# Another plan for the first batch: the flag behind the sums, filters ahead of weights, the last rows stored and read back first, eight weight blocks beside the first units

## The chip, the cores and the metric

The kernel runs on one core of a Trainium2 chip. The metric is the device time of one execution in microseconds (us), the median of three runs. The engines are named as the profile names them: PE is TensorE (matmuls), PEld its weight loads, DVE is VectorE, ACT is ScalarE, POOL is GpSimd, SP is SyncE, which issues nearly all DMAs here. Every engine works through its own list of instructions in order.

## The reference

Two stages, of which the second does most of the arithmetic:

```python
X = np.fft.rfft(x, axis=1)                    # x: 8 x 3008 x 256
y = np.fft.irfft(X * F, n=3008, axis=1)       # F: 1505 x 256, complex
h = y.reshape(24064, 256) @ w_in              # 256 x 2048
P = a[0] + a[1]*h + a[2]*h**2 + a[3]*h**3
Q = 1.0 + abs(b[0])*abs(h) + abs(b[1])*h**2
out = (P / (Q + 1e-06)) @ w_out               # 2048 x 256
```

All in float32 (the weights come as float64 bits that the kernel decodes itself). The kernel keeps float32 accuracy by splitting each operand in a high and a low part, so that one product takes three matmuls.

## The kernel before, in words

**Units.** The second stage is cut into token tiles of 512 and, in each, 16 slices of 128 of the 2048 inner columns. A pair of tile and slice is a unit; there are 752, and the last two are split. `pipeline` writes the program one unit index `i` after the other: `product_in` of unit i (six matmuls on PE, `h_u`), then its scalar functions on ACT (`act0` to `act4`), the sums on DVE (`p`, `g_hi`, `rest`, `g_lo`), two steps on POOL (`pool_q1`, `pool_m`), each with a lag in units (`ORDER`), and `product_out` of unit i-4 (six matmuls, `o`). Under the flag of the `if`, which holds for these inputs, the branch with `squares` runs.

**Convolution.** The Fourier stage of a batch is done as small DFTs. `conv_items(b)` is a generator: `stage1` (matmuls `s`), then `stage2`, whose twelve items each have a forward product `y` on PE, two multiplications with the filter on DVE, `cross` and `total`, `halves` (the split `zr`, high part on ACT, low part on POOL) and an inverse product `z` on PE, which ACT evicts to `ev`. `zr` has a single buffer. Finished quarters go to a scratch in HBM (`scr2`), and `stage3` reads chunks of it back (`tl`), multiplies by `e_sb` (matmuls `x`) and writes `xhl`, the tokens for the units. In `pipeline` a counter `credit` grows by `RATES[0]` = 0.6 a unit while batch 1 is made and by 0.38 later, and an item costs 0.86. `SPN` = 1 is the unit from which batch 1 may begin. A chunk of the batch that is still being made forces the rest of that batch at once:

```python
need = chunks[xk][0]
if c1 <= t * T + RX and ((c0 if f > XF else c1) < T * (t + 2) or need < nxt):
    if need >= nxt:
        run(gen or conv_items(nxt))
```

The first chunk of batch 1 comes up at unit 73 (tile 4, slice 9).

**Head.** Batch 0 is done ahead of the units by `head`, whose steps a small planner (`Plan`) puts in order: each step has an engine, a cost, the steps that it needs and a due time, and the planner takes the one that can begin first. Steps: loads `x0` to `x6`; `sum` (DVE) and `s` (PE); the flag (some twenty tiny POOL operations, its bits written by a DVE operation) and the reciprocals; for each of six filters a load, `sign` (POOL or ACT), `swb` (ACT), two `y`, `mul` (two DVE operations each), `z` and an eviction; stores `zst`; the read-back `tl`; and the decoding of the weight blocks in `FIRST`. A block is decoded by `magnitude` and, if in `EASED`, `scale` on ACT, four DVE operations (`guard`, `shift`, `top`, `power`), `rest` (POOL if eased, else DVE), `whole` (POOL), `upper` (ACT), `lower` (POOL). Twelve of the sixteen blocks are in `FIRST`; four are decoded beside the units listed in `LATE`. All engines take the branch of the `if` only after their part of the head.

Of the kernel before, what the change touches and what calls it, by code (L numbers as in the profile page):

```python
# [53 lines left out]
RAW = {10: "f1", 11: "f2", 14: "f1", 15: "oe"}  # L54
LATE = {0: 10, 3: 11, 6: 14, 9: 15}
# [66 lines left out]
class Plan:  # L122
# [60 lines left out]
def conv_moe(ctx: ExitStack, tc: tile.TileContext, xp, filt, w_in, w_out, mats, small, sgn, outT):  # L183
# [36 lines left out]
    def load_flag():  # L220
# [24 lines left out]
        v.tensor_tensor(out=flag_sb, in0=all_[:, :1], in1=all_[:, :1], op=ALU.mult)  # L245

    def recip_scalars():

        ts, tt = nc.gpsimd.tensor_scalar, nc.gpsimd.tensor_tensor
        yes, no = scal[:, 54:55], scal[:, 55:56]  # L250
        n, r, z, half = scal[:, :7], scal[:, 56:63], cf_sb[:, 8:15], scal[:, 63:64]
# [9 lines left out]
        v.reciprocal(r, n)  # L261
# [249 lines left out]
    class Stage2:  # L511
# [17 lines left out]

        def sign_filter(self, q, by):  # L530
            f1 = self.f[q][0]
            for k in range(4):
                out, sg = f1[64:, k], sgn_sb[64:, 4 * q + k : 4 * q + k + 1]
                if by == "A":
                    nc.scalar.activation(out, out, AF.Copy, scale=sg)
                else:
                    nc.gpsimd.tensor_scalar(out=out, in0=out, scalar1=sg, scalar2=1.0, op0=ALU.mult, op1=ALU.mult)

        def swap_filter(self, q):
            f1, f2 = self.f[q]  # L540
            nc.scalar.activation(f2[:64], f1[64:], AF.Copy)
# [128 lines left out]
    class Unit:  # L670
# [137 lines left out]
    def head():  # L808
# [30 lines left out]

        def s_sum(j):  # L840
# [320 lines left out]
```

## Time and profile before

| what | value |
|---|---|
| median of three runs | 2470.52 us (2466.96 to 2471.79) |
| the profiled execution's own time | 2470.01 us |
| its span, first to last instruction | 2468.2 us |
| PE, DVE, ACT, POOL busy | 98%, 89%, 91%, 87% |

The span is 1.8 us shorter than the execution's own time. PE is busy nearly throughout, and the four engines are all near their limits, so the time is read from the stretches in which PE is not busy.

### The profile page before, as it was taken

What the parts mean: (1) busy time and instruction counts of PE and PEld (TensorE: products, weight loads), DVE (VectorE), ACT (ScalarE), POOL (GpSimd) and SP (SyncE); (2) the same over time, 40 slices, a digit from 0 to 9 for tenths busy, and PEclk for the clock granted to TensorE, in tenths of its full rate; (3) what the DMA queues carried; (4) which work ended last, traced back from release to release, by engine and by line L of the source; (5) the groups of instructions that cost most, each with busy time, mean ns of one, the idle gap of its engine ahead of it and who ended that gap; (6) DMA issues with size and microseconds to landing.
All of it is one profiled execution on the core that took longest, in us unless ns stands there. A gap on an engine that the chain in (4) does not pass through costs nothing.

```text
span 2468.2 us, 36873 instructions
## 1 busy us (share of the span) xinstructions
PE 2419.6 (98%) x10868; PEld 1953.5 (79%) x10868; DVE 2197.2 (89%) x3571; ACT 2237.4 (91%) x4285; POOL 2147.6 (87%) x2245
## 2 busy tenths in 40 slices
PE   8799999999999999999999999999999999999998
PEld 4578877888788887888788877888788888888886
DVE  7789988989899888998899988899889998998997
ACT  6799999999999999999999999999999999888887
POOL 7888987999879987899879997899879987888897
PEclk9999999999999999999999999999999999999999
DMA  8554334432443233433343233432343210100000
GB/s 285 153 179 146 99 119 132 136 99 77 126 151 111 89 101 109 153 94 98 111 141 119 87 98 120 136 111 89 106 133 109 70 38 17 34 26 17 21 9 19
DMA packets 131698, 251.16 MB, mean 102 GB/s; under 512 B 10958, under 2 KB 78862, under 8 KB 131486
## 3 DMA queue, kind: packets, MB, share of 16 engines
q1 hardware_dynamic: 131486, 248.70, 32.3%
q8 instruction: 88, 1.44, 0.2%
q14 instruction: 124, 1.02, 0.1%
HBM read 154.12 MB, written 94.54 MB: 101 GB/s over the span
## 4 chain that ended last, share of the span: by engine, by line
PE 69%; POOL 15%; DVE 7%; issue 4%; ACT 3%; DMA 2%; SPq 0%; POOLq 0%; ACTq 0%; DVEq 0%
PE o L769 10%; PE o L770 10%; PE o L771 10%; PE h_u L689 10%; PE h_u L692 10%; PE h_u L690 10%; POOL q_u L751 6%; POOL q_u L732 4%; PE s L504 3%; PE x L648 3%; POOL zw L575 2%; DVE h_u L754 2%; PE z L414 2%; DVE hi_u L746 1%; PE y L414 1%
## 5 line engine op out<-in xcount | busy, mean ns | idle before, releaser
L751 POOL TENSOR_TENSOR q_u<-q_u,hi_u 128x512 f32<-128x512 f32 x753 | 976.5, 1297 | 197.9 <-DVE hi_u L746 175.3
L754 DVE SCALAR_TENSOR_TENSOR h_u<-h_u,q_u 128x512 f32<-128x512 f32 x753 | 521.3, 692 | 121.9 <-POOL q_u L751 120.9
L769 PE MATMUL o<-hi_u,wo_sb 128*128 128x512 f32 x1506 | 629.2, 418 | 0.0
L689 PE MATMUL h_u<-xhl,wi_sb 128*128 128x512 f32 x1506 | 591.1, 393 | 10.8 <-DVE xhl L664 5.4
L770 PE MATMUL o<-lo_u,wo_sb 128*128 128x512 f32 x1506 | 588.0, 390 | 3.2 <-DVE lo_u L760 3.2
L690 PE MATMUL h_u<-xhl,wi_sb 128*128 128x512 f32 x1506 | 586.6, 390 | 0.7 <-DVE xhl L664 0.7
L771 PE MATMUL o<-hi_u,wo_sb 128*128 128x512 f32 x1506 | 586.8, 390 | 0.0
L732 POOL TENSOR_SCALAR q_u<-q_u,scal 128x512 f32<-128x512 f32 x753 | 580.6, 771 | 2.9 <-ACT a_u L714 2.9
L697 ACT ACTIVATE q_u<-h_u 128x512 f32<-128x512 f32 x753 | 450.7, 599 | 131.8 <-PE h_u L692 104.1
L737 DVE SCALAR_TENSOR_TENSOR h_u<-w_u,scal,h_u 128x512 f32<-128x512 f32 x753 | 561.6, 746 | 0.0
L760 DVE TENSOR_TENSOR lo_u<-h_u,a_u 128x512 fp32r<-128x512 f32 x753 | 514.4, 683 | 0.1
L746 DVE SCALAR_TENSOR_TENSOR hi_u<-h_u,a_u 128x512 fp32r<-128x512 f32 x753 | 512.4, 680 | 1.7 <-ACT a_u L722 1.4
L714 ACT ACTIVATE a_u<-q_u 128x512 f32<-128x512 f32 x753 | 477.8, 635 | 0.0
L710 ACT ACTIVATE q_u<-q_u 128x512 f32<-128x512 f32 x753 | 473.0, 628 | 1.8
L692 PE MATMUL h_u<-xhl,wi_sb 128*128 128x512 f32 x1506 | 464.2, 389 | 0.0
L704 ACT ACTIVATE w_u<-h_u 128x512 f32<-128x512 f32 x753 | 446.1, 592 | 0.0
L722 ACT ACTIVATE a_u<-a_u 128x512 f32<-128x512 f32 x688 | 432.5, 629 | 0.3
L689 PEld LDWEIGHTS h_u<-xhl,wi_sb 128*128 128x128 f32 x1506 | 283.1, 188 | 80.0 <-DVE lo_u L760 15.3
L770 PEld LDWEIGHTS o<-lo_u,wo_sb 128*128 128x128 f32 x1506 | 283.6, 188 | 76.2 <-issue 17.3
L769 PEld LDWEIGHTS o<-hi_u,wo_sb 128*128 128x128 f32 x1506 | 283.3, 188 | 72.2 <-issue 18.4
L771 PEld LDWEIGHTS o<-hi_u,wo_sb 128*128 128x128 f32 x1506 | 283.0, 188 | 60.1
L690 PEld LDWEIGHTS h_u<-xhl,wi_sb 128*128 128x128 f32 x1506 | 283.2, 188 | 59.4 <-DVE xhl L664 1.1
(107 smaller groups left out, 2291.2 us busy)
## 6 DMA issues: line engine op xcount, KB each, us to landing
f<-filt SPq DMA_DIRECT2D x174, 256.0 KB
xin<-xp SPq DMA_DIRECT2D x48, 512.0 KB
scr<-ev SPq DMA_DIRECT2D x48, 512.0 KB
outT<-oe SPq DMA_DIRECT2D x46, 512.0 KB
xin<-scr SPq DMA_DIRECT2D x42, 512.0 KB
yl<-scr SPq DMA_DIRECT2D x42, 512.0 KB
scr<-xin SPq DMA_DIRECT2D x42, 480.0 KB
scr<-yl SPq DMA_DIRECT2D x42, 480.0 KB
```

What stands on the lines that cost most here:

```text
L689: nc.tensor.matmul(o, w_in_part(0, f, cc), xh[:, cc, ts], start=cc == 0, stop=False)
L690: nc.tensor.matmul(o, w_in_part(0, f, cc), xl[:, cc, ts], start=False, stop=False)
L692: nc.tensor.matmul(o, w_in_part(1, f, cc), xh[:, cc, ts], start=False, stop=cc == 1)
L732: nc.gpsimd.tensor_scalar(out=self.q, in0=self.q, scalar1=S1, scalar2=S2, op0=ALU.mult, op1=ALU.add)
L737: v.scalar_tensor_tensor(out=H, in0=w, scalar=PK, in1=H, op0=ALU.add, op1=ALU.mult)
L746: nc.vector.scalar_tensor_tensor(out=self.hi, in0=self.H, scalar=self.p0, in1=self.a, op0=ALU.add, op1=ALU.mult)
L751: nc.gpsimd.tensor_tensor(out=self.q, in0=self.q, in1=self.hi.bitcast(F32), op=ALU.mult)
L754: nc.vector.scalar_tensor_tensor(out=self.H, in0=self.H, scalar=self.p0, in1=self.q, op0=ALU.add, op1=ALU.subtract)
L760: nc.vector.tensor_tensor(out=self.lo, in0=self.H, in1=self.a, op=ALU.mult)
L769: nc.tensor.matmul(o, w_out_part(0, f, dd), self.hi, start=f == 0 and self.cols.start == 0, stop=False)
L770: nc.tensor.matmul(o, w_out_part(0, f, dd), self.lo, start=False, stop=False)
L771: nc.tensor.matmul(o, w_out_part(1, f, dd), self.hi, start=False, stop=f == 15 and self.cols.stop == T)
```

## The change

The planner's costs and due times are set anew, the flag's bits and the reciprocals become steps of their own on DVE behind the last sum, all filters are loaded as early as their tiles allow (filter 3 gets tiles of its own), and the last quarter's rows are stored in two parts, of which the first twelve of each half go first and are read back first. Eight weight blocks are decoded in the head and eight beside units 1 to 15, where `pool_q1` of the first twelve units moves from POOL to ACT. The convolution of batch 1 may begin at unit 14 (`START`), and the first chunk of `stage3` in `pipeline` is not taken at unit 1 any more. The diff, cut to its core:

```diff
-FIRST = (0, 1, 4, 5, 2, 3, 8, 9, 6, 7, 12, 13)
+FIRST = (0, 1, 4, 5, 2, 3, 8, 9)
-EASED = (0, 1, 4, 2, 8, 6, 7, 12, 10, 11, 14, 15)
+EASED = (0, 1, 4, 5, 2, 8, 6, 7, 12, 13, 10, 11, 14, 15)
+OWN = {3: 16}
+START = 14
-SOON = {0: (10, 11, 14, 15)}
+SOON = {0: (6, 7, 12, 13, 10, 11, 14, 15)}
-LATE = {0: 10, 3: 11, 6: 14, 9: 15}
+LATE = {1: 6, 3: 7, 5: 12, 7: 13, 8: 10, 10: 11, 11: 14, 13: 15}
+Q1A = 12
+DUE = 5
...
-        v.tensor_tensor(out=flag_sb, in0=all_[:, :1], in1=all_[:, :1], op=ALU.mult)
+    def flag_bits():
+        v.tensor_tensor(out=flag_sb, in0=scal[:, 54:55], in1=scal[:, 54:55], op=ALU.mult)
...
+    def stage3_load(k, k0=0, k1=K2, tl=None, issuers=(nc.sync,)):
...
         def pool_q1(self):
-            if self.squares:
+            if self.squares and self.i < Q1A:
+                nc.scalar.activation(self.q, self.q, AF.Identity, scale=S1, bias=S2)
+            elif self.squares:
                 nc.gpsimd.tensor_scalar(out=self.q, in0=self.q, scalar1=S1, scalar2=S2, op0=ALU.mult, op1=ALU.add)
...
+        def load_filter(q):
+            if q in OWN:
+                tiles = [mlp.tile([128, TT], F32, tag=slots[OWN[q] + n], name=f"fr0_{q}_{n}") for n in range(4)]
...
-        due = lambda i: 18 + 2.6 * i
+        due = lambda i: DUE + 2.6 * i
...
+        add("bits", flag_bits, "DVE", 0.2, ["flag", "sum12"], due=14)
+        add("inputs", recip_inputs, "POOL", 2.0, ["flag"], due=4)
+        add("recips", recips, "DVE", 0.25, ["inputs", "bits"], due=15)
+        add("recip_step", recip_step, "POOL", 0.9, ["recips"], due=4)
...
-            add(f"f{q}", lambda q=q: s.load_filter(q), "SP", 1.0, due=-8 + q if q < 3 else due(2 * q) - 9, moves=1.95, ring=("f1", f"z{2 * q + 1}"), twin="f2")
+            add(f"f{q}", lambda q=q: load_filter(q), "SP", 1.0, ["s12"] if q in OWN else [], due=-8 + q, moves=2.35, ring=None if q in OWN else ("f1", f"z{2 * q + 1}"), twin=None if q in OWN else "f2")
...
+        add("few", lambda: rows(5, 0, 12, (nc.sync, nc.scalar)), "SP", 0.5, ["zev11"], due=-7, moves=0.3)
+        add("zst5", lambda: rows(5, 12, N1, (nc.sync, nc.sync)), "SP", 1.0, ["tr0!", "tr1!"], due=-5, moves=1.3)
...
+        def rows(q, r0, r1, issuers):
+            for e, issuer in enumerate(issuers):
+                p = slice(e * N1 + r0, e * N1 + r1)
+                issuer.dma_start(scr2[0][4 * q : 4 * q + 4, p].rearrange("k p c -> p k c"), s.ev[q][p])
...
+            add(f"tr{k}", lambda k=k: tl_rest(k), "SP", 0.8, [f"tl{k}!", "few", "zst4"], due=-6 + k, moves=0.3)
...
+            decode(i, 0, "magnitude", "scale")
             step(0, "product_in")
...
-            if i < n and f in (XF, XF + 8) and not xgen and xk < len(chunks):
+            if i < n and f in (XF, XF + 8) and i > XF and not xgen and xk < len(chunks):
...
-                if gen is None and nxt < B and i >= SPN and i >= 94 * nxt - 94 - EARLY:
+                if gen is None and nxt < B and i >= START and i >= 94 * nxt - 94 - EARLY:
```

What this does to the order of instructions is shown at three places. The first is DVE at the start, where `xs` are the sums, `xin` the loaded tiles and L245 (L253 in the changed kernel) writes the flag's bits. Before:

```order
L447 TENSOR_TENSOR xs_124<-xin_0_109 120x512 [waits DMAHW0_49]
L447 TENSOR_TENSOR xs_128<-xin_0_109 120x512
L245 TENSOR_TENSOR scal<-scal 128x1 [waits Pool_49]
L447 TENSOR_TENSOR xs_166<-xin_1_112 120x512 [waits DMAHW2_49]
L447 TENSOR_TENSOR xs_180<-xin_1_112 120x512
```

And now, at the end of the sums:

```order
L462 TENSOR_TENSOR xs_292<-xin_6_122 120x256 [waits DMAHW7_49]
L462 TENSOR_TENSOR xs_292<-xin_6_122 120x256
L253 TENSOR_TENSOR scal<-scal 128x1 [waits Pool_49]
L271 RECIPROCAL scal<-scal 128x7 [waits Pool_49]
L925 TENSOR_TENSOR f_0_152<-y_0_344,f_0_152 128x512 [waits DMAHW2_49,PE_49,Activation_49]
```

The operation that waits for POOL stood behind the second sum and now stands behind the fourteenth, ahead of the first multiplication with a filter.

The second place is SP's list behind filter 2, where `f` and `fr` are filters, `raw` weight blocks and `scr` the scratch. Before:

```order
L524 DMA f_2_213<-filt 64x1024 [waits DMAHW1_49]
L329 DMA raw_350<-w_in 128x1024 [waits DMAHW2_49,DVE_49]
L329 DMA raw_361<-w_in 128x1024 [waits DMAHW3_49,DVE_49]
L329 DMA raw_373<-w_out 128x1024 [waits DMAHW4_49,DVE_49]
L1085 TENSOR_LOAD scal [waits DVE_49]
L1085 ISA x2
L329 DMA raw_388<-w_out 128x1024 [waits DMAHW5_49,DVE_49]
L329 DMA raw_399<-w_in 128x1024 [waits DMAHW6_49,DVE_49]
L329 DMA raw_420<-w_in 128x1024 [waits DMAHW7_49,DVE_49]
L523 DMA f_3_426<-filt 128x1024 [waits DMAHW0_49,PE_49,Activation_49]
```

And now:

```order
L863 DMA f_2_200<-filt 64x1024 [waits DMAHW1_49]
L1148 TENSOR_LOAD scal [waits DVE_49]
L1148 ISA x2
L858 DMA fr_3_0_335<-filt 128x512 [waits DMAHW2_49,DVE_49,PE_49]
L859 DMA fr_3_2_337<-filt 64x512 [waits DMAHW3_49,DVE_49,PE_49]
L858 DMA fr_3_1_336<-filt 128x512 [waits DMAHW4_49]
L859 DMA fr_3_3_338<-filt 64x512 [waits DMAHW5_49,DVE_49,PE_49]
L344 DMA raw_398<-w_in 128x1024 [waits DMAHW6_49]
L862 DMA f_4_410<-filt 128x1024 [waits DMAHW7_49,PE_49,Activation_49]
```

Six weight blocks stood between filters 2 and 3; now none does, and one stands between filters 3 and 4.

The third place is PE's list at unit 73, where `y` and `z` are products of batch 1 with the item's number behind the name, `h_u` is a unit's `product_in` and `o` a `product_out`. Before, the last item of batch 1 stands in unit 72 between products of units:

```order
L692 MATMUL h_u_3388<-xhl,wi_sb 128x512 x2
L414 MATMUL z_11_3395<-zr_11_3376,inv_sb 128x512 x3
L769 MATMUL o_0_3322<-hi_u_3289,wo_sb 128x512
L770 MATMUL o_0_3322<-lo_u_3352,wo_sb 128x512
L771 MATMUL o_0_3322<-hi_u_3289,wo_sb 128x512
```

And now, in unit 73:

```order
L702 MATMUL h_u_3361<-xhl,wi_sb 128x512 x2
L429 MATMUL y_9_3372<-xin_4_2932,fwd_sb 128x512 x2
L429 MATMUL y_9_3372<-yl_4_2933,fwd_sb 128x512
L429 MATMUL z_8_3382<-zr_8_3368,inv_sb 128x512 x3
L429 MATMUL y_10_3393<-xin_5_3158,fwd_sb 128x512 x2
L429 MATMUL y_10_3393<-yl_5_3159,fwd_sb 128x512
L429 MATMUL z_9_3402<-zr_9_3390,inv_sb 128x512 x3
L429 MATMUL y_11_3414<-xin_5_3158,fwd_sb 128x512 x2
L429 MATMUL y_11_3414<-yl_5_3159,fwd_sb 128x512
L429 MATMUL z_10_3424<-zr_10_3410,inv_sb 128x512 x3
L429 MATMUL z_11_3435<-zr_11_3432,inv_sb 128x512 x3
L781 MATMUL o_0_3253<-hi_u_3267,wo_sb 128x512
```

Seven products of batch 1, three `y` and four `z`, now stand one behind the other with no unit's matmul between them; from unit 74 on both lists have the same items at the same units.

## Rows read from the trace of the kernel before

**Rows 1.** The page: each engine's busy time, share of the span, instructions.

```profile
PE 2419.6 (98%) x10868; PEld 1953.5 (79%) x10868; DVE 2197.2 (89%) x3571; ACT 2237.4 (91%) x4285; POOL 2147.6 (87%) x2245
```

**Rows 2.** Windows: stretch, length, each engine's busy time (instructions), granted clock, DMA.

```profile
73.20:123.20 50.00, 35.80 (x150) 26.73 (x148) 37.42 (x62) 38.52 (x74) 41.07 (x37) 0.93 0.57 148
123.20:331.00 207.80, 205.69 (x902) 164.65 (x901) 186.68 (x303) 199.95 (x390) 186.21 (x189) 1.00 0.45 142
80.00:90.00 10.00, 3.81 (x22) 3.03 (x22) 5.68 (x9) 9.97 (x20) 5.72 (x6) 1.00 1.03 274
50.00:60.00 10.00, 8.00 (x15) 3.44 (x16) 10.00 (x17) 7.32 (x14) 7.15 (x7) 0.83 0.40 142
```

**Rows 3.** Timeline of the start: start, duration, engine, line, [idle before, releaser].

```profile
9.78 0.16 DVE L245 TENSOR_TENSOR scal<-scal 128x1 int32<-128x1 f32 x1 [4.38 <-POOL scal L244]
9.85 6.79 DVE L447 TENSOR_TENSOR xs<-xin 120x512 f32<-120x512 f32 x12
10.59 3.63 POOL L260 TENSOR_SCALAR scal<-small_sb,scal 128x4 f32<-128x4 f32 x2
11.21 10.90 PE L854 MATMUL s<-small_sb,xs 120*64 120x120 f32 x174 [0.18 <-DVE xs L447]
13.54 0.43 SPq L329 DMA_DIRECT2D raw<-w_in  x1
17.69 0.20 POOL L264 TENSOR_TENSOR scal<-scal 128x7 f32<-128x7 f32 x1
24.52 0.68 DVE L886 TENSOR_TENSOR f<-y,f 128x512 f32<-128x512 f32 x1
```

**Rows 4.** Timeline of batch 0's filters and last inverse product.

```profile
21.92 1.86 POOL L537 TENSOR_SCALAR f<-f,sgn_sb 64x256 f32<-64x256 f32 x4 [2.06 <-DMA f<-filt]
46.77 1.86 POOL L537 TENSOR_SCALAR f<-f,sgn_sb 64x256 f32<-64x256 f32 x4 [1.56 <-DMA f<-filt]
61.47 6.17 PE L872 MATMUL warm<-still 128*128 128x512 f32 x14
```

**Rows 5.** Timeline from the last store of batch 0 to ACT's first unit.

```profile
63.60 0.38 SPq L600 DMA_DIRECT2D scr<-ev  x1
70.87 2.58 PE L648 MATMUL x<-small_sb,tl 120*128 120x141 f32 x20 [3.23 <-DMA tl<-scr]
78.22 0.63 ACT L389 ACTIVATE wi_sb<-wt 128x512 fp32r<-128x512 f32 x1 [0.64 <-POOL wt L386]
79.98 0.60 ACT L697 ACTIVATE q_u<-h_u 128x512 f32<-128x512 f32 x1 [1.13 <-PE h_u L692]
```

**Rows 6.** Timeline of the first units: `g_hi` of unit 0, and PE.

```profile
85.40 0.68 DVE L746 SCALAR_TENSOR_TENSOR hi_u<-h_u,a_u 128x512 fp32r<-128x512 f32 x1
91.14 0.79 PE L689 MATMUL h_u<-xhl,wi_sb 128*128 128x512 f32 x1 [4.83 <-DVE xhl L664]
96.85 0.43 PE L690 MATMUL h_u<-xhl,wi_sb 128*128 128x512 f32 x1
```

**Rows 7.** Timeline of items 10 and 11 of batch 1, units 69 to 72.

```profile
313.90 0.62 PE L414 MATMUL y<-xin,fwd_sb 128*128 128x512 f32 x2
317.78 0.94 PE L414 MATMUL z<-zr,inv_sb 128*128 128x512 f32 x3 [0.88 <-DVE f L560]
319.17 0.63 ACT L407 ACTIVATE ev<-z 128x512 f32<-128x512 f32 x1
319.82 0.90 ACT L573 ACTIVATE zw<-f,sgn_sb 64x256 f32<-64x256 f32 x2
320.81 1.30 POOL L579 TENSOR_TENSOR f<-f,zw 128x512 f32<-128x512 f32 x1 [0.44 <-ACT zw L573]
323.40 0.62 ACT L585 ACTIVATE zr<-f 128x512 fp32r<-128x512 f32 x1
324.10 1.29 POOL L586 TENSOR_TENSOR zr<-f,zr 128x512 fp32r<-128x512 f32 x1
325.36 0.84 PE L414 MATMUL z<-zr,inv_sb 128*128 128x512 f32 x3
```

More of the change, by code (lines that the diff above doesn't have):

```diff
@@ L167, in run @@
             self.end[name] = end + 0.12
+            self.end[name + "!"] = self.free[engine]
             if bank:
@@ L910, in head @@
         add = plan.add
-        due = lambda i: 18 + 2.6 * i
+        due = lambda i: DUE + 2.6 * i
         for t in range(7):
-            add(f"x{t}", lambda t=t: x_load(t), "SP", 0.5, due=-20 + t, moves=1.3 if t < 6 else 0.65, ring=(("xin", "xin", "xin", "xin", "oe", "oe", "tl")[t], f"sum{min(2 * t + 1, 12)}"))
+            add(f"x{t}", lambda t=t: x_load(t), "SP", 0.5, due=-20 + t, moves=1.55 if t < 6 else 0.78, ring=(("xin", "xin", "xin", "xin", "oe", "oe", "tl")[t], f"sum{min(2 * t + 1, 12)}"))
@@ L920, in head @@
+        add("mats_upper", mats_upper, "ACT", 0.97, ["pair", "sev12"], due=45)
+        add("mats_lower", mats_lower, "POOL", 1.5, ["mats_upper"], due=50)
         for j in range(13):
-            add(f"sum{j}", lambda j=j: s_sum(j), "DVE", 0.6, [f"x{j // 2}"], due=j)
+            add(f"sum{j}", lambda j=j: s_sum(j), "DVE", 0.61 if j < 12 else 0.75, [f"x{j // 2}"], due=j)
             need = [f"sum{min(2 * (j // 2) + h, 12)}" for h in range(2)]
-            add(f"s{j}", lambda j=j: s_mm(j), "PE", 0.88, need + ["small"], due=j, bank=f"sev{j}")
@@ L924, in head @@
-            add(f"sev{j}", lambda j=j: s_ev(j), "ACT", 0.47, [f"s{j}"], due=j)
+            add(f"s{j}", lambda j=j: s_mm(j), "PE", 0.86, need + ["small"], due=j, bank=f"sev{j}")
+            add(f"sev{j}", lambda j=j: s_ev(j), "ACT", 0.56, [f"s{j}"], due=j)
         add("abs", load_abs, "ACT", 0.2, ["small"], due=3)
         add("flag", load_flag, "POOL", 8.0, ["abs"], due=3)
-        add("recips", recip_scalars, "POOL", 3.0, ["flag"], due=4)
+        add("bits", flag_bits, "DVE", 0.2, ["flag", "sum12"], due=14)
@@ L934, in head @@
+            add(f"sign{q}", lambda q=q: sign_filter(q, SIGN[q]), "POOL" if SIGN[q] == "P" else "ACT", 2.05 if SIGN[q] == "P" else 1.75, [f"f{q}", "mats"], due=due(2 * q) - 5)
+            add(f"swb{q}", lambda q=q: swap_filter(q), "ACT", 1.2 if q in OWN else 1.03, [f"sign{q}"], due=due(2 * q) - 3)
             for i in (2 * q, 2 * q + 1):
                 add(f"y{i}", lambda i=i: y_mm(i), "PE", 0.86, [f"sev{g}" for g in range(13)] + ["pair"], due=due(i), bank=f"mul{i}")
-                add(f"mul{i}", lambda i=i: y_mul(i), "DVE", 1.22, [f"y{i}", f"swb{q}"], due=due(i) + 1)
+                add(f"mul{i}", lambda i=i: y_mul(i), "DVE", 1.3, [f"y{i}", f"swb{q}"], due=due(i) + 1)
@@ L1065, in pipeline @@
                 step(lag, name)
-            for lag, names in enumerate((("magnitude", "scale", "guard", "shift"), ("top", "power", "rest", "whole"), ("upper", "lower"))):
-                if i - lag in LATE:
-                    for name in names:
-                        getattr(weights[LATE[i - lag]], name)()
+            decode(i, 0, "guard", "shift", "top", "power")
+            decode(i, 1, "rest", "whole")
+            decode(i, 2, "upper", "lower")
             if ready is not None:
```

130 lines of the change are left out of this document (76 added, 54 removed).

## The prediction

> **What bounds the kernel now.** I read the busy times first [rows 1]: PE is busy 98% of the span, so the question is where PE is not. The windows answer [rows 2]: between 123.2 and 331 us PE works 205.7 of 207.8 us, and I take that on to unit 73 and beyond as "gapless"; between 73.2 and 123.2 it is busy 35.8 of 50 us, and the records overlap. Counted by instructions it did less: of 150 matmuls there, 34 belong to `stage3` (20 of them took 2.58 us [rows 5], so 0.13 each, 4 us) and 116 to units at 0.23 us (207.8 us by 902 instructions [rows 2]), 27 us; together 31 us of work in 50. Behind the point where PE becomes gapless nothing but PE's own work counts, and that is the same in both kernels. So the time changes by what PE stands still (or runs slowly) until unit 74; from there the two lists agree. My measure is the time of a point minus PE's unit work up to it. Before: 123.2 - 31 = 92 us.
>
> **Start.** The bits of the flag hold DVE for 4.38 us, after which twelve sums run without a pause from 9.85 to 16.64 [rows 3]. Their inputs had long landed: SP has eight transfers under way at most, so its issue at 13.54 says that the seventh `xin` was there [rows 3]. With the bits behind, a sum follows its tile, the last at about 14.5. PE then needs its 174 matmuls in 10.9 us [rows 3] from about 7.5 on, so `s` ends near 18.5 instead of 22.1.
>
> POOL gets in the way. Its tiny operations take 0.2 us while DVE waits, but two of them took 3.63 us beside the sums [rows 3], 1.8 each. Now DVE is busy from 7.8 to 14.5, so some five operations crawl, ten follow at 0.25, and POOL is free at about 18.3 instead of 17.9. By the Trainium skill (SBUF — State Buffer, "Summary: rules for kernel authors") a VectorE operation with two SBUF inputs and a GpSimd operation that reads SBUF block each other, the later one until the earlier ends. The trace agrees in kind; by one whole sum of 0.6 us per tiny operation POOL would be free at about 17.5, 0.8 us sooner than I take it.
>
> Behind it come `sign` (1.9 us), `swb` (1.05) and the first multiplication at 21.3, where it stood at 24.52 [rows 3]: 3 us gained.
>
> **Products of batch 0.** Before, filters came late: POOL waited for one at 46.77 [rows 4], with six weight blocks ahead of it in SP's list. Now filter 3 follows filter 2. Filter 1 landed at 21.9 [rows 4]; behind it, at 274 GB/s [rows 2], 1.28 MB (256 KB of its own, a weight block, 512 KB of filter 2) land in 4.7 us, at 26.6, and filter 3 at about 30, ahead of its turn. So DVE is the bound: 24 multiplications and 17 decoding steps stand ahead of the last `z`, at 0.6 us each (17 in 10 us [rows 2]) plus some 2 us of waits: 21.3 + 24.6 + 2, then 1.7 for `z`: 49.6. Before, the last `z` gave way to the `warm` matmuls at 61.47 [rows 4]. Gain so far 12 us.
>
> **Store, read-back, decoding.** ACT's eviction of the last `z` stands behind an `upper` that waits for POOL: 51.3. Store to first `x` took 7.27 us [rows 5]; the pieces are smaller and one more hop of the same kind remains, so I keep 7: `x` at 58.3, its evictions until 61.5. POOL's decoding is as long: 22 operations of 1.3 us [rows 7] for the eight blocks, from 28.5 on (`sign` of filter 2 behind its landing), 1.9 us for `sign` of filter 4 with a wait of some 1.5 for its landing, and 4 us for turns in which `lower` waits for ACT's `upper`: 64.5, the last `upper` a step before, at 63. ACT enters the units about 1.1 us after it (78.85 to 79.98 [rows 5]): at 64.2 instead of 79.98. Bounds: 62.7, if the read-back alone decides, and 68, if every `lower` waits.
>
> **First units.** Before, unit 0's `g_hi` came 5.4 us after ACT's first operation [rows 5, 6]; now 69.6. Eight blocks instead of four lie beside the units. For the thirteen units to `g_hi` of unit 13 ACT has five operations each, twelve `pool_q1`, some 21 decoding steps and two evictions, 100 at 0.5 us (20 in 10 us [rows 2]): 50 us. DVE has 52 operations of units, 28 of decoding and two of `stage3`, 82 at 0.6: 49 us. POOL has 35 of 1.3: 45 us. No engine reaches its sum when three are that full; I add 4 us: `g_hi` of unit 13 at 124, and PE gapless from about 126. The stand of PE before unit 3 (4.83 us, waiting for a chunk's eviction [rows 6]) is gone, as that chunk now comes at unit 10; convolution, which fills PE's gaps, is gone there too, since batch 1 starts at unit 14.
>
> At 126 PE has done 17 `product_in`, 12 `product_out` and one chunk: 174 x 0.23 + 2 = 42 us. 126 - 42 = 84: against 92, **8 us gained**. Bounds: 3 (ACT at 68, or 10% lost to turns) and 14 (ACT at 62.7, nothing lost).
>
> **Unit 73.** `RATES` is left as it was, and batch 1 starts thirteen units later. Its items then end later by as much, but the first chunk of batch 1 is still due at unit 73, and there the generator is run to its end: seven products in a row. Before, an item's parts lay among units, and its waits cost PE nothing. In a row, `zr` has one buffer and ACT evicts a `z` ahead of the next item's `zw`, so each item is a circle: `z` 0.94, `ev` 0.63, `zw` 0.90, `total` 1.30, `zr` on ACT 0.62, on POOL 1.29 [rows 7], with 0.05 to 0.1 us at each of six hand-overs 6.0 us. From the first `y` it takes about 2.4 us to `z` of item 8 (ACT's and POOL's halves of that item, 0.62 and 1.29, behind the units' work), then three circles and a last `z`: 2.4 + 18 + 0.9 = 21.3 us, in which PE does 21 matmuls, 4.8 us. **PE stands still 16.5 us**, and since it was the bound on either side, that is lost.
>
> Then the clock. After the stand that ended at 91.14 PE's matmuls came 0.43 us apart until 96.85, and 0.23 behind that [rows 6]: the lower of the two levels for thirteen of them, 2.6 us lost. The three stands here, of some five us each, are as long; I take one such loss, 2.6 us, between none and one behind each. By the Trainium skill (TensorE: Matmul & The Clock Gate, "HAM oscillation — how this bites in real kernels") an engine that works in short runs between long waits falls back before each run. By that, the three `z` would take 0.6 us more each as well, and the sum would be 1.8 us higher; no row here shows stands that follow each other so closely. Bounds for unit 73: 13 (PE's list ahead of the other engines by one circle's half) and 21.5 (lower clock throughout). What the stand might hide: nothing else is late there, as PE has units' work waiting on both sides.
>
> Refill behind it: `product_out` of 69 to 71 and `product_in` of 74 to 76 are ready or need one bank each, 8 us of work, in which ACT, DVE and POOL bring unit 72 to its end: no further loss. The store and read-back of 7.3 us fit there too.
>
> **Sum.** -8 + 16.5 + 2.6 = +11. The profiled execution took 2470.0 us, 0.5 below the median; I forecast 2480 us against the median of 2470.5.
>
> **Rivals.**
> *About the same.* The head gives 11 to 14 us, or unit 73 costs 13 to 15, and the two cancel: 2467 to 2475. It decides where ACT's first unit comes before 63 us and thirteen units take under 52 us. For it: my three sums for the units (50, 49, 45) lie below what I take; against it: in 73.2 to 123.2, where four blocks were decoded, no engine was over 82% busy [rows 2], so turns cost more than I add.
> *Faster.* The first units run at PE's pace: 13 units in 36 us at 12 x 0.23 = 2.74 each, not 54, because decoding fits in gaps. Then the gain is 8 + 18 = 26, and unit 73 takes 19 back: 2463. It decides below 2.9 us per unit (38 us). Against it stands ACT's count, 100 operations at 0.5 us.
> *The head does not shorten.* POOL's turns and the split store cost as much as the filters gain, ACT enters at 70 or later, and unit 73 comes on top: 2487 to 2490. For it: POOL is the longest list and each `lower` waits for ACT.
>
> **How the numbers follow.** Forecast (slower by 5 to 17 us) 0.64, head not shorter 0.10, same 0.19, faster 0.07. A measurement of this kernel can tell about 0.2%, 5 us, from no change: slower 0.74, same 0.19, faster 0.07. The range: the ends of both terms give -14 + 13 = -1 and -3 + 21.5 = +18.5; I take 2469 to 2488, which leaves the rivals' far ends, some 0.15, outside.
>
> **What would show it.** DVE's sums without a wait for POOL; first multiplication near 21; last `z` near 50; `x` near 58; ACT's first unit operation near 64; `g_hi` of unit 13 near 124; then, some 60 units on, near 325 us, PE idle between products of batch 1 for 16 us in three to four pieces, and the same order of work behind it. The prediction is wrong if PE's stand there is under 10 us in all, or if the units start before 60.

## The result and the profile after

The changed kernel takes 2488.36 us (median of four runs, 2487.43 to 2491.21), the kernel before 2470.11 (four runs): a ratio of 1.0077, interval 1.006 to 1.0095, or 19 us slower. The direction was forecast; the size (2480, range 2469 to 2488) was too small. The profiled execution took 2488.14 us, its span is 2486.2.

The busy times, which answer to [rows 1], show PE and ACT busier by some 10 us each (PE's list has the same length; ACT has twelve `pool_q1` more), DVE and POOL hardly changed:

```profile
PE 2429.9 (98%) x10868; PEld 1956.2 (79%) x10868; DVE 2193.1 (88%) x3569; ACT 2248.6 (90%) x4300; POOL 2143.5 (86%) x2235
```

Windows of the changed kernel, the first two the same stretches as in [rows 2], the third around unit 73:

```profile
73.20:123.20 50.00, 36.39 (x126) 26.97 (x124) 38.83 (x63) 44.79 (x84) 33.15 (x27) 0.76 0.34 84
123.20:331.00 207.80, 199.12 (x870) 157.30 (x869) 182.55 (x298) 191.07 (x372) 181.08 (x180) 1.00 0.43 132
326.31:349.46 23.15, 11.48 (x25) 6.04 (x24) 6.36 (x11) 9.05 (x18) 16.36 (x19) 0.63 0.51 155
350.00:2400.00 2050.00, 2039.89 (x9146) 1663.32 (x9145) 1842.56 (x2994) 1885.12 (x3596) 1793.13 (x1868) 1.00 0.30 94
```

In the first, PE did 126 matmuls where it did 150 before, at a granted clock of 0.76; from 123.2 to 331 it worked 199 us where it worked 206; around unit 73 it did 25 matmuls in 23 us. From 350 us on it works 99.5% of the time again. So two places differ, the first units and unit 73.

**The head** came at the times forecast. Its timeline (start, duration, engine, line, idle before):

```profile
7.91 6.96 DVE L462 TENSOR_TENSOR xs<-xin 120x512 f32<-120x512 f32 x12 [2.56 <-DMA xin<-xp]
14.78 0.16 DVE L253 TENSOR_TENSOR scal<-scal 128x1 int32<-128x1 f32 x1
9.26 9.23 PE L893 MATMUL s<-small_sb,xs 120*64 120x120 f32 x174 [0.18 <-DVE xs L462]
17.39 1.86 POOL L873 TENSOR_SCALAR f<-f,sgn_sb 64x256 f32<-64x256 f32 x4
20.99 0.69 DVE L925 TENSOR_TENSOR f<-y,f 128x512 f32<-128x512 f32 x1 [4.58 <-ACT f L877]
51.11 6.17 PE L911 MATMUL warm<-still 128*128 128x512 f32 x14
58.21 2.58 PE L658 MATMUL x<-small_sb,tl 120*128 120x141 f32 x20 [0.94 <-DMA tl<-scr]
65.81 0.60 ACT L707 ACTIVATE q_u<-h_u 128x512 f32<-128x512 f32 x1 [1.17 <-issue]
70.86 0.68 DVE L758 SCALAR_TENSOR_TENSOR hi_u<-h_u,a_u 128x512 fp32r<-128x512 f32 x1
132.73 0.67 DVE L758 SCALAR_TENSOR_TENSOR hi_u<-h_u,a_u 128x512 fp32r<-128x512 f32 x1
```

The sums run through, `s` ends at 18.49, the first multiplication is at 20.99, the last `z` gives way at 51.11, `x` comes at 58.21, ACT's first unit at 65.81 and `g_hi` of unit 0 at 70.86; forecast were 18.5, 21.3, 49.6, 58.3, 64.2 and 69.6. The last row is `g_hi` of unit 13: 132.73 for a forecast 124. Up to unit 0 the prediction's times are good to 2 us; from there to unit 13 they are 7.5 us short (61.9 us for 54.4).

**The first units.** Among the longest waits between 60 and 130 us (engine, line, what for: us in total, times, longest), and the rows in which PE waits for the weight decoding, with DVE and ACT around the last of them:

```profile
PE h_u L699 <- DVE wp L378: 11.9, 3, 5.6
DVE xhl L674 <- ACT xhl L672: 10.1, 3, 4.4
POOL q_u L763 <- DVE hi_u L758: 8.0, 2, 6.3
PE o L782 <- DVE lo_u L772: 7.0, 5, 2.2
```

```profile
70.54 0.79 PE L699 MATMUL h_u<-xhl,wi_sb 128*128 128x512 f32 x1 [3.24 <-DVE wp L378]
94.83 0.76 PE L699 MATMUL h_u<-xhl,wi_sb 128*128 128x512 f32 x1 [3.05 <-DVE wp L378]
107.66 0.65 DVE L674 TENSOR_TENSOR xhl<-x,xhl 128x470 fp32r<-128x470 f32 x1 [4.11 <-ACT xhl L672]
112.35 0.80 PE L699 MATMUL h_u<-xhl,wi_sb 128*128 128x512 f32 x1 [5.60 <-DVE wp L378]
115.31 0.60 ACT L707 ACTIVATE q_u<-h_u 128x512 f32<-128x512 f32 x1 [3.32 <-PE h_u L702]
117.79 0.65 DVE L674 TENSOR_TENSOR xhl<-x,xhl 128x470 fp32r<-128x470 f32 x1 [4.44 <-ACT xhl L672]
```

PE's three rows are `product_in` of units 4, 8 and 11. By the program's order each takes the PSUM bank in which a late block's magnitude lay, and so waits until DVE has got through that block's `top` (L378), the last step that reads the bank. The rows show a ring: at 107.66 DVE has waited 4.11 us for ACT's half of a chunk's eviction; behind it stand the unit's sums and the decoding steps up to `top`; only then comes PE's `product_in` (112.35), for which ACT waits 3.32 us before it can begin the next unit (115.31); and DVE waits for ACT again at the chunk's second half (117.79).

PE was not gapless behind unit 13 either. Its window from 125 us on:

```profile
125.00:160.00 35.00, 31.28 (x135) 23.72 (x136) 30.15 (x49) 30.09 (x59) 32.34 (x30) 1.00 0.33 90
```

It lacks 3.7 us there, for `lo_u` of DVE most of all; before, it was busy 34.73 us of the same stretch.

**Unit 73.** PE from the first `y` of the forced run to the first unit's matmul behind it:

```profile
325.86 0.62 PE L429 MATMUL y<-xin,fwd_sb 128*128 128x512 f32 x2
...
327.22 0.73 PE L429 MATMUL z<-zr,inv_sb 128*128 128x512 f32 x2 [0.53 <-ACT zr L583]
329.66 0.50 PE L429 MATMUL z<-zr,inv_sb 128*128 128x512 f32 x1 [1.70 <-POOL zr L584]
330.00 0.63 PE L429 MATMUL y<-xin,fwd_sb 128*128 128x512 f32 x2
...
333.84 2.15 PE L429 MATMUL z<-zr,inv_sb 128*128 128x512 f32 x3 [2.98 <-ACT zr L583]
335.78 1.06 PE L429 MATMUL y<-xin,fwd_sb 128*128 128x512 f32 x2
...
339.66 2.15 PE L429 MATMUL z<-zr,inv_sb 128*128 128x512 f32 x3 [2.40 <-ACT zr L583]
345.48 2.15 PE L429 MATMUL z<-zr,inv_sb 128*128 128x512 f32 x3 [3.67 <-ACT zr L583]
347.42 0.63 PE L781 MATMUL o<-hi_u,wo_sb 128*128 128x512 f32 x1
347.85 0.63 PE L782 MATMUL o<-lo_u,wo_sb 128*128 128x512 f32 x1
...
349.69 0.39 PE L699 MATMUL h_u<-xhl,wi_sb 128*128 128x512 f32 x1
```

The circle of one item is 5.82 us (333.84, 339.66, 345.48), forecast 6.0, and from the first `y` to the end of the last `z` it is 21.8 us, forecast 21.3. From the first `y` to `product_in` of unit 74 (349.69) are 23.8 us, in which PE does 27 matmuls, 6.2 us at 0.228 us each (205.7 us by 902 [rows 2]). Read at the place itself, the run costs 17.7 us.

**A ledger.** To set kernels side by side I read when `product_in` of unit 40 and of unit 80 begins: unit 40 lies behind the start-up and ahead of unit 73, unit 80 behind both. In the trace of before and in that of the changed kernel:

```profile
218.79 0.39 PE L689 MATMUL h_u<-xhl,wi_sb 128*128 128x512 f32 x1
...
349.31 0.39 PE L689 MATMUL h_u<-xhl,wi_sb 128*128 128x512 f32 x1
...
2459.41 0.28 PE L771 MATMUL o<-hi_u,wo_sb 128*128 128x256 f32 x1
```

```profile
219.16 0.39 PE L699 MATMUL h_u<-xhl,wi_sb 128*128 128x512 f32 x1
...
369.49 0.39 PE L699 MATMUL h_u<-xhl,wi_sb 128*128 128x512 f32 x1
...
2480.24 0.28 PE L783 MATMUL o<-hi_u,wo_sb 128*128 128x256 f32 x1
```

Ahead of unit 40, kernels that begin batch 1 at unit 14 have done five products of batch 1 (15 matmuls, 3.4 us at 0.228) fewer, which follow before unit 80; so 3.4 us are added for them. The changed kernel is then 219.16 + 3.4 - 218.79 = 3.8 us late at unit 40, and 20.2 us at unit 80, so 16.4 us are lost in between. That is less than the 17.7 us at the place itself, because the changed kernel made up some 2 us on the way: `product_in` of unit 73 comes at 324.50 for 327.40 before, 2.9 us earlier, but with 21 matmuls (4.8 us) fewer done, so it is 1.9 us late. Its last matmul comes 20.8 us later than before, the span ends only 18.0 later, since the profile of before goes on for 8.5 us behind its last matmul and this one for 5.7; in the other profiles this was between 5.6 and 8.3 us, and nothing here explains it.

### The profile page after: what moved, and what is told of

Its sections match the earlier page's. It is cut to its first block, busy times and chain, and to the rows that moved or that the text cites. A ratio compares the mean times of both kernels' runs of the same rounds, so it can differ in the third digit from the quotient of the medians.

```text
span 2486.2 us, 36867 instructions
## 1 busy us (share of the span) xinstructions
PE 2429.9 (98%) x10868; PEld 1956.2 (79%) x10868; DVE 2193.1 (88%) x3569; ACT 2248.6 (90%) x4300; POOL 2143.5 (86%) x2235
## 4 chain that ended last, share of the span: by engine, by line
PE 67%; POOL 17%; DVE 7%; issue 5%; ACT 3%; DMA 1%; SPq 0%; POOLq 0%; ACTq 0%; DVEq 0%
PE o L782 10%; PE o L781 10%; PE o L783 10%; PE h_u L699 10%; PE h_u L702 9%; PE h_u L700 9%; POOL q_u L763 7%; POOL q_u L744 4%; PE x L658 3%; PE s L519 3%; POOL zw L573 2%; DVE h_u L766 2%; POOL zr L584 2%; DVE hi_u L758 1%; DVE h_u L749 1%
## 5 line engine op out<-in xcount | busy, mean ns | idle before, releaser
L782 PEld LDWEIGHTS o<-lo_u,wo_sb 128*128 128x128 f32 x1506 | 284.4, 189 | 87.2 <-issue 18.5
L699 PEld LDWEIGHTS h_u<-xhl,wi_sb 128*128 128x128 f32 x1506 | 283.8, 188 | 87.7 <-DVE lo_u L772 15.4
```

What stands on the lines that cost most here:

```text
L699: nc.tensor.matmul(o, w_in_part(0, f, cc), xh[:, cc, ts], start=cc == 0, stop=False)
L782: nc.tensor.matmul(o, w_out_part(0, f, dd), self.lo, start=False, stop=False)
```

## The experiments

"Late at 40" and "late at 80" are against the kernel before, in the profiled executions, 3.4 us added at 40 where batch 1 begins at 14. The ratio is that of the timed runs to the kernel before on the same chip. One execution of each kernel was profiled. How far single executions differ shows in ACT's first unit, which the changed kernel's own head (all of its variants but e5 and e7) reached between 65.46 and 68.90; a difference of less than some 3 us between two traces can be of that kind.

| kernel | ACT's first unit | late at 40 | late at 80 | ratio (interval) |
|---|---|---|---|---|
| before | 79.98 | 0 | 0 | 1 |
| changed | 65.81 | 3.8 | 20.2 | 1.0077 (1.006 to 1.0095) |
| e1_start1 | 68.90 | 10.6 | 10.6 | 1.0037 (1.0023 to 1.0051) |
| e2_before_start14 | 79.70 | -0.6 | 15.4 | 1.0059 (1.0046 to 1.0073) |
| e3_q1_pool | 67.71 | 3.2 | 20.1 | 1.0075 (1.0061 to 1.0089) |
| e4_scratch_sbuf | 65.81 | 8.2 | 25.2 | 1.0104 (1.0088 to 1.0119) |
| e5_head_only | 85.61 | 6.0 | 6.0 | 1.0035 (1.0022 to 1.0047) |
| e6_batch1_unit6 | 66.51 | 7.9 | 7.9 | 1.007 (1.0056 to 1.0084) |
| e7_flag_first | 67.95 | 5.2 | 21.8 | 1.0081 (1.0068 to 1.0095) |
| e8_no_late_decode | 66.79 | -10.4 | 6.8 | 1.0029 (1.0018 to 1.0039) |
| e9_one_dve_step | 66.69 | 0.2 | 17.2 | 1.006 (1.0043 to 1.0077) |
| e10_no_pool_rest | 65.46 | 0.4 | 17.2 | 1.0065 (1.0049 to 1.0082) |
| e11_before_eleven | 76.92 | 0.0 | 0.0 | 1.0007 (0.9998 to 1.0016) |
| e12_before_ten | 75.69 | 1.2 | 1.2 | 1.0009 (0.9999 to 1.0018) |

**e1: batch 1 from unit 1.**

```diff
-START = 14
+START = 1
```

> The changed kernel with batch 1 begun at unit 1 again, so that no product of batch 1 is left for unit 73. Theory (two terms: unit 73 cost 17 us of the changed kernel, its first units gave nothing back but lost 3): the stand at unit 73 is gone, 2488 - 17 = 2471 us, at most 2 us more where the convolution's evictions lengthen ACT's list in units 8 to 17, at most 4 less where its matmuls lie in PE's gaps there. Rival (unit 73 is a shift only, and the changed kernel is slow for the whole of its first units): above 2478 us.

Measured 2476.83 us beside 2468.09 for before, 9 us slower by ratio. That is 2479 on the 2470.11 of before from which the two theories count, so in the rival's range; but the trace contradicts the rival's mechanism, by which unit 73 is a shift only. Nothing more is lost between 40 and 80: the run at unit 73 is gone, as the theory has it. But at unit 40 this kernel is 10.6 us late, 6.8 more than the changed one, so the theory's price for the convolution among the first units (at most 2) was wrong. It begins `s` in unit 8, where late blocks are decoded; the kernel before, with its first chunk at units 2 and 3, began `s` in unit 12. Between 112 and 150 us its longest waits are (same columns as above):

```profile
POOL q_u L763 <- DVE hi_u L758: 11.4, 4, 4.4
ACT xin L478 <- PE s L519: 6.1, 3, 2.9
DVE xhl L674 <- ACT xhl L672: 6.0, 2, 3.8
DVE yl L479 <- ACT xin L478: 5.4, 5, 2.2
```

The evictions of `s` (`xin`, `yl`) now stand in the same ring as the chunk's. Against a start of `s` in unit 8, the late start of batch 1 is worth 6.8 us at the first units, and it costs 16.4 at unit 73.

**e2: the kernel before, batch 1 from unit 14.**

```diff
-                if gen is None and nxt < B and i >= SPN and i >= 94 * nxt - 94 - EARLY:
+                if gen is None and nxt < B and i >= 14 and i >= 94 * nxt - 94 - EARLY:
```

> The kernel before, with one number changed: batch 1 may begin at unit 14 instead of 1. Theory (the forced run at unit 73 costs 17 us by itself, whatever the head is): 2470 + 17 = 2487 us, between 2484 and 2489, with PE idle in three pieces of 3 to 4 us near 330 us. Rival (the forced run hurts only behind the new first units, or the start of batch 1 beside the first units cost as much as it now gives back): under 2480 us.

Measured 2483.55 us, some 15 above before (2484.7 by ratio, in the theory's range); the trace is 15.9 us later at 80 than at 40. PE waits as in the changed kernel:

```profile
328.62 0.82 PE L414 MATMUL z<-zr,inv_sb 128*128 128x512 f32 x2 [2.88 <-ACT zr L585]
...
334.44 2.15 PE L414 MATMUL z<-zr,inv_sb 128*128 128x512 f32 x3 [2.40 <-ACT zr L585]
340.26 2.15 PE L414 MATMUL z<-zr,inv_sb 128*128 128x512 f32 x3 [3.67 <-ACT zr L585]
```

The forced run is a loss by itself, whatever the head. (The rate has no part in it: the program's order is the same for any `RATES[0]` from 0.5 to 0.8. An item takes three turns, and a unit gives one turn.)

**e3: `pool_q1` on POOL.**

```diff
-Q1A = 12
+Q1A = 0
```

> The changed kernel with pool_q1 of the first twelve units on POOL again. Theory (ACT's list is the bound of units 0 to 10: 114 operations of 0.54 us to g_hi of unit 13): twelve steps of 0.71 us leave it, 8.5 us, POOL takes up 12 x 0.77 = 9.2 us and has 23 us of room, so g_hi of unit 13 comes 5 to 8 us earlier and the time is 2481 to 2484 us. Rival (the PSUM banks that the weight decoding takes set the pace, and ACT is full only because it has work waiting): within 2 us of 2488.

Measured 2487.44 us, within 1 us of the changed kernel by ratio; 0.6 us earlier at unit 40. ACT was busy 61.4 us of the 68 from 65 to 133 in the changed kernel, and yet 8.5 us less for it gave 0.6 us, or 2.5 counted from ACT's first unit, which came 1.9 us later in this execution. `g_hi` of unit 13 came at 132.14 for 132.73, and not 5 to 8 us earlier: the theory that ACT's list is the bound falls.

**e4: the late blocks' scratch in SBUF.**

```diff
-            self.bank, self.a = banks.tile(f"wa{self.i}")
+            if self.i in FIRST:
+                self.bank, self.a = banks.tile(f"wa{self.i}")
+            else:
+                self.room()
+                self.a = self.t.bitcast(F32)
...
```

> The changed kernel with the magnitude of the eight late weight blocks in an SBUF tile that the block has anyway, not in a PSUM bank. Theory of ACT's list: no work leaves ACT, so 2486 to 2489 us, although PE's stands of 3.2, 3.1 and 5.6 us behind a decoding step of DVE (before product_in of units 4, 8 and 11) shrink. Rival (banks): those three stands set the pace, 4 to 8 us are gained, 2480 to 2484 us.

Measured 2493.45 us, slower than the changed kernel, which neither theory had. The stand ahead of unit 4 vanished (its `product_in` came at 67.23 for 70.54), but `product_in` of unit 5 stayed at 78.39: PE only waited for `lo_u` in its place. Unit 11 was 4.1 us earlier, unit 16 5.8 us later, for two new reasons: the tile is taken earlier, so ACT waits for POOL's `lower` of the block that had it (3.38 us at 109.39), and DVE's steps with all operands in SBUF wait beside POOL:

```profile
124.16 0.43 DVE L389 TENSOR_SCALAR wp<-wp 128x512 uint32<-128x512 uint32 x1
...
129.40 1.67 DVE L368 SCALAR_TENSOR_TENSOR wp<-wp,raw 128x512 f32<-128x512 f32 x1
131.10 1.40 DVE L373 TENSOR_SCALAR wp<-wp 128x512 uint32<-128x512 uint32 x1
...
133.73 1.37 DVE L389 TENSOR_SCALAR wp<-wp 128x512 uint32<-128x512 uint32 x1
```

So the experiment doesn't weigh the banks alone. It shows that without them PE stands at the next wait of the ring.

**e5: the new head, everything else as before** (with the tables that follow from the two lists).

```diff
-FIRST = (0, 1, 4, 5, 2, 3, 8, 9)
+FIRST = (0, 1, 4, 5, 2, 3, 8, 9, 6, 7, 12, 13)
-START = 14
+START = 1
-LATE = {1: 6, 3: 7, 5: 12, 7: 13, 8: 10, 10: 11, 11: 14, 13: 15}
+LATE = {0: 10, 3: 11, 6: 14, 9: 15}
-Q1A = 12
+Q1A = 0
...
```

> The changed kernel's head (flag behind the sums, filters ahead of weights, rows stored in two parts) with the other parts as before: twelve weight blocks in the head, four beside units 0, 3, 6 and 9, pool_q1 on POOL, batch 1 from unit 1. Theory (the four blocks that were moved out of the head are paid for in full among the units, and the head's new order is a gain of its own): ACT enters its first unit 3 to 8 us sooner than before (72 to 77 us for 80), nothing is left for unit 73, and the time is 2462 to 2468 us, 3 to 8 below the kernel before. Rival (POOL's decoding sets the head's end, whatever the order of filters and flag): ACT's first unit within 2 us of 80, the time within 3 us of the kernel before.

Measured 2477.14 us beside 2469.23: slower than before, which neither theory had. With twelve blocks the head's decoding ends later than in the old order:

```profile
81.48 0.63 ACT L404 ACTIVATE wi_sb<-wt 128x512 fp32r<-128x512 f32 x1 [3.07 <-POOL wt L401]
82.72 0.63 ACT L404 ACTIVATE wi_sb<-wt 128x512 fp32r<-128x512 f32 x1 [0.61 <-POOL wt L401]
...
85.61 0.58 ACT L707 ACTIVATE q_u<-h_u 128x512 f32<-128x512 f32 x1
```

The last `upper` waits for POOL and comes at 82.72, where it stood at 78.22 [rows 5]; ACT enters 5.6 us later, PE is 6.0 us late at unit 40. Twelve blocks' decoding sets the head's end, and the last `z` (gives way at 52.34 for 61.47) and `x` (62.19 for 70.87), some nine us earlier, gain nothing. POOL ends its part of the head 4.5 us later, and its waits there, from 17 us on, add up to 16.5 us for 12.3 before; the longest are 3.8 for the landing of filter 2 and 3.1 for an `upper` of ACT. (Two more things differ from before: the first chunk in `pipeline` comes at unit 10 and not at unit 2, and `s` of batch 1 begins in unit 8 and not in unit 12.)

**e6: batch 1 from unit 6 with shorter pauses.**

```diff
-GAP = 4
+GAP = 2
-START = 14
+START = 6
-REST = 4
+REST = 1
```

> The changed kernel with batch 1 begun at unit 6 and with two of its pauses shortened (one turn for four before the first sums, two for four before stage2): first product s in unit 12 (unit 8 where batch 1 began at unit 1, unit 23 in the changed kernel), last z in unit 72, nothing left for unit 73. Theory (two separate prices: 16 us for the run at unit 73, and 7 us for a convolution whose first products lie in units 8 to 17): the first is gone, the second mostly too: 2471 to 2475 us. Rival (the start of stage1 costs the same 7 us wherever it lies among units whose weights are still being decoded, up to unit 15): as with a start at unit 1, 2476 to 2478 us.

Measured 2486.29 us, above both. Up to unit 80 its trace is 7.9 us late, the value of a start of `s` in unit 12, between e1 (10.6) and the changed kernel (3.8); the rest, some 12 us, comes in later batches, whose pause `GAP` shortens too (12.4 us late at unit 150, 19.6 at unit 400). Its total therefore says nothing on the two theories; its first 80 units lie between them, nearer to the rival.

**e7: the flag's bits ahead of the sums again.**

```diff
-        add("flag", load_flag, "POOL", 8.0, ["abs"], due=3)
-        add("bits", flag_bits, "DVE", 0.2, ["flag", "sum12"], due=14)
+        add("flag", lambda: (load_flag(), flag_bits()), "POOL", 8.0, ["abs"], due=3)
...
```

> The changed kernel with the flag's bits written where they stood before, behind the second sum. Theory (3 us of the head come from this): the first multiplication with a filter near 24 us instead of 21, the units start 2 to 3 us later; but of the 12 us that the units started earlier nothing was left by unit 20, so the time is the same as the changed kernel's within 1.5 us (2486 to 2489). Rival (the head's lead is passed on to the end): 2490 to 2492 us.

Measured 2488.99 us, a ratio of 1.0081 for 1.0077, as the theory has it; 1.4 us later at unit 40. The first multiplication comes at 24.62 for 20.99, 3.6 us later, the last `z` gives way at 53.82 for 51.11, 2.7 later, and ACT's first unit is at 67.95, 2.1 later, and within the 65.46 to 68.90 of the other executions. Behind the head, the flag's place makes no difference that can be told from none.

**e8: no decoding beside the units.** Of each late block's ten steps only two ACT copies of raw numbers are left:

```diff
                 if i - lag in LATE:
                     for name in names:
-                        getattr(weights[LATE[i - lag]], name)()
+                        if name == "upper":
+                            w = weights[LATE[i - lag]]
+                            for n in range(2):
+                                nc.scalar.activation(w.parts[:, n], w.h.bitcast(F32), AF.Copy)
```

> The changed kernel without the decoding of the eight weight blocks beside the units: of their ten steps only two ACT copies of raw numbers are left (DVE's four and POOL's three steps and ACT's scale and magnitude are left out), so its output is not the reference's. Unit 73 stays as it is. Theory (what the late blocks cost is the whole of the lost lead): the first units keep most of the 12.6 us by which they start earlier, PE is gapless 10 to 16 us sooner than in the changed kernel, 2472 to 2478 us. Rival (the units' own start, with its chunk and its low clock, eats the lead): 2484 to 2488 us.

Measured 2477.33 us, in the theory's range; 14.2 us earlier than the changed kernel at unit 40. Here ACT is the bound, busy without a gap while POOL is half idle:

```profile
80.00:140.00 60.00, 52.41 (x227) 41.10 (x226) 43.45 (x70) 60.00 (x115) 29.25 (x26) 0.97 0.34 94
```

**e9 and e10: one engine's part left out.** e9 drops three of DVE's four steps of each late block and frees the PSUM bank behind the first, e10 drops POOL's `rest` and `whole`:

```diff
...
-                        getattr(weights[LATE[i - lag]], name)()
+                        if name not in ("shift", "top", "power"):
+                            getattr(weights[LATE[i - lag]], name)()
...
-                        getattr(weights[LATE[i - lag]], name)()
+                        if name not in ("rest", "whole"):
+                            getattr(weights[LATE[i - lag]], name)()
```

> The changed kernel with one DVE step for each of the eight late blocks instead of four (shift, top and power left out, so the output is not the reference's); ACT's and POOL's steps stay. That takes 24 DVE operations, some 15 us, from DVE and frees the block's PSUM bank sooner. Theory (DVE's order decides: PE stands behind a decoding step of DVE or behind lo_u): 6 to 10 us gained, 2478 to 2482 us. Rival (ACT and POOL carry the pace, DVE only waits with them): 0 to 2 us, 2486 to 2488.

> The changed kernel with POOL's rest and whole left out for the eight late blocks (the output is not the reference's), DVE's four steps, ACT's three and POOL's lower stay: 16 POOL operations, some 21 us, less, and upper no longer waits for POOL. Theory of DVE's order: 0 to 3 us gained, 2485 to 2488 us. Rival (POOL's part of each block, and the ACT step that waits for it, carry the pace): 6 to 10 us gained, 2478 to 2482.

Measured 2485.11 and 2486.16 us, at unit 40 3.6 and 3.4 us earlier than the changed kernel. e9 lies between its two theories; e10 is at the edge of the range for DVE's order (0 to 3 us). Taking 15 us from DVE or 21 from POOL gives the same 3.5, and 8.5 from ACT gave 0.6 (e3), while the whole is worth 14.2 (e8): none of these parts is the bound by itself. e10's gain also lies late: up to `product_in` of unit 17 it is 0.5 us ahead of the changed kernel at most (136.40 for 136.87), at unit 19 2.9 (141.84 for 144.72). That the lists wait for each other in a ring is read from the rows of the changed kernel above; no run took out the parts of two engines together, so how the 14.2 us divide stays open.

**e11 and e12: the kernel before with eleven and ten blocks in the head.**

```diff
-FIRST = (0, 1, 4, 5, 2, 3, 8, 9, 6, 7, 12, 13)
+FIRST = (0, 1, 4, 5, 2, 3, 8, 9, 6, 7, 12)
-LATE = {0: 10, 3: 11, 6: 14, 9: 15}
+LATE = {0: 13, 2: 10, 4: 11, 7: 14, 10: 15}
...
+FIRST = (0, 1, 4, 5, 2, 3, 8, 9, 6, 7)
+LATE = {0: 12, 2: 13, 4: 10, 6: 11, 8: 14, 10: 15}
...
```

> The kernel before with eleven weight blocks in the head instead of twelve; five are decoded beside units 0, 2, 4, 7 and 10. Batch 1 begins at unit 1 as before, nothing is left for unit 73. Theory (four late blocks cost PE nothing, eight cost 14.7 us, about 3.7 for each above four, as much as POOL's three steps of 1.3 us save in the head): within 2 us of the kernel before. Rival (there is room for a fifth block among the units): ACT enters its units 3 to 4 us sooner and 2 to 4 us are gained.

> The kernel before with ten weight blocks in the head; six are decoded beside units 0, 2, 4, 6, 8 and 10. Theory (each block above four costs among the units what it saves in the head): within 3 us of the kernel before, though ACT's first unit comes 5 to 8 us sooner. Rival (room for two more blocks): 4 to 7 us gained. Second rival (turns among the engines cost more with every block): 3 to 8 us slower.

Measured 2469.88 and 2472.78 us beside 2469.44: the same. ACT enters 3.1 and 4.3 us sooner, and at unit 40 PE is 0.0 and 1.2 us late. The theory holds: what a block saves in the head it costs among the units. No version beat the kernel before.

## Why the prediction was wrong

**Unit 73: right, a little too large.** Forecast 16.5 of stands and 2.6 of clock, 19.1 in all; measured 17.7 at the place itself, 16.4 in the ledger and 15.9 in e2. The split was off: PE's stands in the rows are 0.53 + 1.70 + 2.98 + 2.40 + 3.67 = 11.3 us, the rest is matmuls at the lower clock (granted 0.63 in this stretch; 0.43 us apart from 347.42 to 348.70, 0.23 from 349.46) and `z` products that stretch over POOL's half of `zr`. The stands are shorter because slow matmuls fill a part of the circle. The rule of the Trainium skill weighed there (TensorE: Matmul & The Clock Gate, "HAM oscillation — how this bites in real kernels") has the clock fall before each short run. The trace agrees, as far as the clock was low in all three runs behind the long stands: the granted clock from 333.84 to 349.40 is 0.50, the lower of the two levels, and matmuls come 0.43 us apart behind the first and the third (rows at 335.78 and 347.42). The 2.15 us of the three `z` products, 0.94 in [rows 7], hold a wait for POOL's half of `zr` too.

**The head: the times right, the reading not.** The forecast had ACT's first unit 15.8 us earlier, measured 14.2, and counted gains of the new order on the way there. e5 shows that the earlier entry came from leaving four blocks out; with twelve the new order enters 5.6 us later. And between the first `y` and the end of the filters, where the prediction says that DVE is the bound, it was PE:

```profile
19.60:51.11 31.51, 31.07 (x73) 13.09 (x72) 26.65 (x45) 28.04 (x63) 20.61 (x26) 1.00 0.99 304
```

PE was busy 31.07 of 31.51 us, DVE 26.65. That DVE's sum and PE's come to nearly the same end, 49.6 forecast and 51.1 measured, is luck. e7 fits: there PE's first `y` comes 3.1 us later (22.70), PE is busy without a gap from it on (31.30 of 31.30 us), and the last `z` gives way 2.7 us later.

**First units: the step that failed.** "No engine reaches its sum when three are that full; I add 4 us: `g_hi` of unit 13 at 124, and PE gapless from about 126", which gave the term of -8. It came out as +3.8: 12 us of error, more than the whole miss. Of the 12 us, 1.3 came from the head, 7.5 were lost up to `g_hi` of unit 13, and some 3 behind it, where PE was not gapless. Two things were wrong. ACT's count left out the units that run ahead of unit 13: in 65.8 to 133 us it had 114 operations, busy 61.4 us, for 100 at 0.5. By its own frame, the longest list plus 4 us, the right count would have given 69.6 + 61.4 + 4 = 135, so the count could pass for the whole cause. But the frame was wrong too, as e3 shows: with 8.5 us less on ACT `g_hi` of unit 13 came 0.6 us earlier, or 2.5 counted from ACT's own entry. In that stretch three engines each hold parts of every unit and every block in one fixed order, and the lists wait for each other: e3, e9 and e10 take 8.5, 15 and 21 us from one engine each, and get 0.6, 3.6 and 3.4 back, where the decoding as a whole is worth 14.2 (e8). The prediction also held PE's stand at the chunk (4.83 us, [rows 6]) to be gone; it came back at units 10 and 11 as waits of DVE for ACT (4.1 us in the row at 107.66, 4.4 the second time) and 5.6 us of PE.

By differences of the ledger at unit 40, the 3.8 us are: new head's order with the old number of blocks +6.0 (e5); four blocks more beside the units and `pool_q1` on ACT +4.6 (e1 less e5); batch 1 begun later -6.8 (changed less e1). With unit 73 that is 6.0 + 4.6 - 6.8 + 16.4 = 20.2. The e5 step holds the moved chunk and the earlier `s` as well, and how much of it is the order of filters and weights was not separated. The -6.8 is against `s` in unit 8; against `s` in unit 12, where the kernel before began it, e6 has -4.1, with shorter pauses. Each step compares two single executions, so it is good to some 3 us.

The rival of a head that does not shorten (2487 to 2490) has the number that came out, by another mechanism: ACT entered at 65.81, not at 70 or later. The rival with units at PE's pace falls: `g_hi` of units 0 to 13 took 70.86 to 132.73, 4.8 us a unit, not 2.74. And the unchanged `RATES`, which the prediction names for the late end of batch 1, is not what holds it: see e2. (The prediction's own terms add up to 11.1 us on 2470.5, which is 2481.6, not 2480; the step that failed is not touched by it.)

## What to carry to other kernels

Preparatory work moved from the head into the first units isn't free just because each engine has some room there: estimate it by what the ring of waits costs when the work is taken out altogether, not by the longest engine's sum, and expect relief of one engine to give back only a fraction. When a producer's start is moved later, look for the deadline at its end: if it is met by running the rest in a row, price one circle through all engines and multiply. And to tell such terms apart, read the start of one and the same instruction at two or three places in every trace. It shows where in the program a difference arises, which whole times can't; but one trace is one execution, and here the same head alone differed by 3.4 us between executions.

## What the runs showed of the hardware

DVE steps on SBUF tiles were held up beside POOL: the same 128x512 step `power` took 0.43 us with POOL idle and 1.37 beside a POOL operation on SBUF (e4, rows at 124.16 and 133.73). `shift` took 0.43 with POOL idle (e4, at 122.97) and 1.40 beside POOL (at 131.10); with its input in PSUM it takes 0.69 in the changed kernel, beside POOL or not. By the Trainium skill (SBUF — State Buffer, "Summary: rules for kernel authors") a VectorE operation in a 2-port mode, or with two SBUF inputs while GpSimd reads SBUF, and a GpSimd operation block each other, and the later waits until the earlier is done. These rows agree with the waiting; no run here shows which mode a step was in.

POOL's tiny operations beside DVE's sums took 0.37 to 0.78 us (0.2 with DVE waiting), not the 1.8 that two of them had suggested [rows 3]; POOL was free at 17.3 for a forecast 18.3. By the Trainium skill (the same section) the prediction had, with one sum of 0.6 us for each, 17.5, which is closer. The stretch from the last matmul to the end of the span varied over fourteen profiles, with one and the same code there, and in two groups: 5.6 to 6.1 us in eight (the changed kernel, e1, e3, e4, e6, e7, e9, e10), 7.6 to 8.5 in six (before, e2, e5, e8, e11, e12). The cause is open.
